# First block's decay factors built as two products outward from its middle, and one transfer of pair 1's x moved to the GpSimd queue

## Chip, cores and metric

One core of a Trainium2 chip runs the whole kernel. The metric is device time in microseconds of one execution; the kernel before has a median of 125.06 us in 3 runs (124.92 to 125.37). One further execution was taken with the hardware profiler, and everything read from the profile below belongs to that one.

## The reference

A chunked state-space scan (4 batches, 8 heads, 768 tokens, head size 32, state size 16) is followed by a bilinear feed-forward layer (3072 tokens, width 256, hidden width 1536). Cut to what matters:

```python
# attention part, chunk by chunk; the state is carried over
cum = np.cumsum(log(a)[chunk]);  L = exp(cum[i] - cum[j]) * causal
y = ((C @ B.T) * L) @ x + (C @ state) * exp(cum)
state = exp(sum(log a)) * state + sum_j B_j x_j exp(cum[-1] - cum[j])
# feed-forward part
x = y.transpose(0, 2, 1, 3).reshape(B * S, H * D)
out = ((x @ w_a) * (x @ w_b)) @ w_out
```

The decay between two tokens of a block is a ratio of running products of `a`, so B is scaled by one factor for each token and head, and C by the inverse of that factor.

## The kernel before

The 768 tokens are cut into six blocks of 128, and each block into two pairs of batches, so there are 12 pairs. For a pair the steps are: scale B and C by their factors (`scale_bc`, giving `bm` and `cm`), turn both on TensorE (`transposes`), copy them out of PSUM (`bt` by ScalarE, `ct` by VectorE or ScalarE), multiply them head by head (`scores`), mask with the causal triangle (`mask`), multiply by the scaled x (`scale_x`, `pv_u`, `pv`), and put the result into `X2T`. Then come the feed-forward products against `Wa` and `Wb` (`units_mm`, `unit`), their product `hk` (`times`) and the output product with `Wo`.

The order on each engine is written out by hand (the schedule is manual): the order of the calls in the program is the order of the instructions on every engine and on every DMA queue. A DMA issued by GpSimd stands between GpSimd's own computing instructions, one issued by SyncE (SP) or ScalarE between theirs. Eight semaphores are used in turn for the DMAs that GpSimd issues, so its ninth DMA waits until its first has landed, and so on.

What lies around the change:

- The first block's factors. `scan(0, 1)` (line 236) multiplies `a` up along 128 tokens for the 32 rows (batch, head), `over_mid` (line 239) takes the inverse of the product at token 63, and `first_factors` (lines 242 and 246) multiplies the two and turns the 32x128 result into token-major order with four turns of 32x64. That gives C's factors (`fC`); their inverse (line 761) gives B's (`fB`).
- The loads at the start. SP and ScalarE load `a`, pair 0's B, C and x. GpSimd issues pair 1's B and C, then `Wa` (first half of its columns, in two transfers: rows `f` = 0 and 1), one half of pair 1's x, and `Wb` in the same two transfers. SP issues the other half of pair 1's x, held back by a manual dependency until the factor inverse at line 761 has run, and then the constant `c32`.
- The warm-up products (line 224): products of a zeroed tile, 11 of them at the start, and some more between the first steps.
- Pair 0's first feed-forward products (line 628): `units_mm` with `Wa` and then with `Wb`, first with the upper 128 features (`f` = 0), then with the lower.
- `hr`, `hs`, `hsx` (lines 830 to 832): the decays of whole blocks, worked out between two `times` calls.

Of the kernel before, what the change touches and what calls it, by code (L numbers as in the profile page):

```python
# [10 lines left out]
f32 = mybir.dt.float32  # L11
# [3 lines left out]
ALU = mybir.AluOpType  # L15
# [14 lines left out]
def kernel(  # L30
# [13 lines left out]
    nc = tc.nc  # L44

    nb, H, S, D = x.shape
    N = B.shape[-1]
    Q = 128
# [50 lines left out]
    NE = P0 // NBP  # L99
    fB = big.tile([128, NE, 2, NBP, H], f32, name="fB")  # L100
    fC = big.tile([128, NE, H + 4 * NBP * H], f32, name="fC")
    Pe = big.tile([BH, 2, 64], f32, name="Pe")
    selr = big.tile([BH, 2, NBP, H], f32, name="selr")
    NL = NBLK - P0 // NBP
    Ps = big.tile([BH, NL, Q], f32, name="Ps")
# [27 lines left out]
    def bank(name):  # L133
        return psf.tile([128, 512], f32, name=name, tag=f"ff{next(banks)}")
# [11 lines left out]
    def load1(eng, p, which, bt, i0=0, n=64):  # L146
        blk, bp = divmod(p, NBP)
        if p >= P0:
            return eng.dma_start(
                by_token(pair_in[p][which])[:, bt],  # L150
                (B, C, x)[which][2 * bp + bt, :, blk * Q : (blk + 1) * Q, :].rearrange("h q n -> q h n"),
            )
        src = (B, C, x)[which][2 * bp + bt, :, blk * Q + 2 * i0 : blk * Q + 2 * i0 + 2 * n, :]
        return eng.dma_start(
            pair_in[p][which][64 * bt + i0 : 64 * bt + i0 + n].rearrange("i h r n -> i h (r n)"),
            src.rearrange("h (i r) n -> i h (r n)", r=2),
        )
# [10 lines left out]
    def load_w(W, t, f=None):  # L168
        src = (moe_w_a if W is Wa else moe_w_b).rearrange("(f p) e -> p f e", p=128)[:, :, t * KC : (t + 1) * KC]
        fs = slice(0, 2) if f is None else slice(f, f + 1)  # L170
        return nc.gpsimd.dma_start(W[t][:, fs], src[:, fs])
# [25 lines left out]
    nc.vector.memset(ident, 1.0)  # L197
    nc.vector.memset(causal, 1.0)
    nc.vector.memset(zero, 0.0)
    nc.vector.memset(hsx, 0.0)  # L200
    nc.vector.memset(causal_q, 1.0)
    nc.vector.memset(c32, 0.0)
    x1 = load1(nc.sync, 1, 2, 0)
    nc.sync.dma_start(c32[0:BH], p32_t.ap())
    nc.gpsimd.affine_select(
        out=ident, in_=ident, compare_op=ALU.is_equal, fill=0.0, base=0, pattern=[[-1, 128]], channel_multiplier=1
    )
# [7 lines left out]
            load1(nc.gpsimd, 1, w, bt)  # L215
    load_w(Wa, 0, 0)
    load_w(Wa, 0, 1)
    load1(nc.gpsimd, 1, 2, 1)
    load_w(Wb, 0, 0)
    load_w(Wb, 0, 1)  # L220

    def warmup(n, bank, reps=4):
        for _ in range(n):
            nc.tensor.matmul(
                bank[:, 0 : 128 * reps],
                warm,
                warm.unsqueeze(1).broadcast_to((128, reps, 128)),
                start=True,
                stop=True,
                skip_group_check=True,  # L230
            )


    def scan(lo, hi):
        for k in range(lo, hi):
            nc.vector.tensor_tensor_scan(Pr[:, k], a_sb[:, k], zero, 1.0, ALU.mult, ALU.add)

    def over_mid(lo, hi):
        nc.vector.reciprocal(rmid[:, lo:hi], Pr[:, lo:hi, 63])

    def first_factors():
        nc.vector.tensor_scalar(Pe, Pr[:, 0].rearrange("p (i r) -> p r i", r=2), rmid[:, 0:1], None, ALU.mult)
        for bt in range(2):
            for c in range(2):
                p0 = 64 * bt + 32 * c
                nc.vector.transpose(  # L246
                    fC[p0 : p0 + 32, 0, H - H * bt : H - H * bt + 64], Pe[:, :, 32 * c : 32 * c + 32]
                )

    def second_sel():  # L250
        nc.vector.tensor_scalar(
# [21 lines left out]
    def f_c(k):  # L273
        return fC[:, k, H : H + 64].rearrange("p (r b t h) -> p r b t h", r=2, b=NBP, t=2)[:, :, :, 0]
# [32 lines left out]
    def scale_bc(p, which, eng, factor=None):  # L307
        blk, bp = divmod(p, NBP)
        name = ("bm", "cm")[which]
        if p >= P0:  # L310
            f = (fBl, fCl)[which][:, blk - P0 // NBP].rearrange("p (b t h) -> p b t h", b=NBP, t=2)[:, bp]
        else:
            f = (f_c(blk) if which else fB[:, blk])[:, :, bp]
        raw = by_token(pair_in[p][which]) if p >= P0 else pair_in[p][which].rearrange("p h r n -> p r h n")
        m_ = pre.tile([128, 2, H, N], f16, name=name, tag=name)
        eng.tensor_tensor(
            out=m_,
            in0=raw,
            in1=(f if factor is None else factor).unsqueeze(3).broadcast_to((128, 2, H, N)),
            op=ALU.mult,  # L320
        )
        st.setdefault(p, {})[name] = m_
    def transposes(p, ps=None, between=None, apart=False):
        s = st[p]
        if p >= P0:
            ps = [bank("tr").bitcast(f16)] * 2
            TB, TC = ps[0][:, 0:256], ps[0][:, 256:512]
            on_dve = False
        elif ps is None:
            ps = [bank("tb") if p == 1 else SC[0], SC[1]] if apart else None  # L330
            on_dve = apart
            TB, TC = (TT[:, 0:256], TT[:, 256:512]) if ps is None else [t_.bitcast(f16)[:, 0:256] for t_ in ps]
        else:
            on_dve = True
            TB, TC = [t_.bitcast(f16)[:, 0:256] for t_ in ps]
        BT = mid.tile([128, 2, 2, 2, 64], f16, name="bt", tag="bt")
        CT = mid.tile([128, 2, Q], f16, name="ct", tag="ct")
        b_ = []

        def turn(T_, src):  # L340
            for r in range(2):
                nc.tensor.transpose(T_[:, r * 128 : (r + 1) * 128], src[:, r].rearrange("p h n -> p (h n)"), ident)  # L342

        def copy_bt(e):
            o_ = BT[:, e].rearrange("p r t i -> p (r t i)")
            b_.append(nc.scalar.activation(out=o_, in_=TB, func=AF.Copy, scale=par[:, e : e + 1]))  # L346

        turn(TB, s["bm"])
        if between:
            between()  # L350
        turn(TC, s["cm"])
        copy_bt(0)
        copy_bt(1)
        if p >= P0:
            nc.scalar.copy(CT.rearrange("p t q -> p (t q)"), TC)
            s["BT"], s["CT"] = BT.rearrange("p e r t i -> p e r (t i)"), CT
            return
        c_ = (nc.vector.tensor_copy if on_dve else nc.scalar.copy)(
            CT.rearrange("p t (i r) -> p r (t i)", r=2), TC.rearrange("p (r c) -> p r c", r=2)
        )  # L360
        if apart:
            for i_ in b_:
                tc.declare_no_dep(c_.ins, i_.ins.name, reason="reads of two banks")
        s["BT"], s["CT"] = BT, CT
# [54 lines left out]
    def mask(out_in, by_pool=False):  # L419
        o_, i_, c_ = out_in  # L420
        if by_pool:
            tmp = mid.tile([128, *c_.shape[1:]], f32, name="tmp", tag="tmp")
            nc.scalar.copy(tmp, i_)  # L423
            nc.gpsimd.tensor_tensor(out=o_, in0=tmp, in1=c_, op=ALU.mult)  # L424
        else:
            nc.vector.tensor_tensor(out=o_, in0=i_, in1=c_, op=ALU.mult)  # L426
# [198 lines left out]
    def units_mm(p, k2s, W, ps, f, ks):  # L625
        for j in ks:
            k2, t_, kk = k2s[j // 2], ps[j // 2], j % 2
            nc.tensor.matmul(  # L628
                t_[:, kk * 2 * Q : (kk + 1) * 2 * Q],
                w_up(W, 2 * k2 + kk, f),  # L630
                X2T[:, p, :, f],
                start=(f == 0 and kk == 0),
                stop=(f == 1),
                skip_group_check=True,
            )
# [117 lines left out]
    def pull(p):  # L753
        if ("S", p) in st:
            st[p].update(st.pop(("S", p)))

    warmup(11, SC[3])
    scan(0, 1)
    over_mid(0, 1)
    first_factors()  # L760
    f0 = nc.vector.reciprocal(fB[:, 0, :, 0], f_c(0)[:, :, 0])
    tc.add_manual_dep(x1.ins, f0.ins.name, AFTER, reason="x of pair 1 behind x of pair 0")
    scale_bc(0, 0, nc.vector)
    scale_bc(0, 1, nc.vector)
    scan(1, 2)
    tb, tcp = bank("tb"), bank("tc")
# [14 lines left out]
    mask(product0(1, 0))  # L781
    mask(product0(1, 1))
    scale_bc(1, 1, nc.gpsimd)
    load_w(Wa, 1)
    load_w(Wb, 1)
    nc.gpsimd.affine_select(
        out=causal_q, in_=causal_q, compare_op=ALU.is_ge, fill=0.0, base=0, pattern=[[1, Q]], channel_multiplier=-1
    )
    warmup(4, tb)
    py = [bank("py0"), bank("py1")]  # L790

# [1 line left out]
    for bt in range(2):  # L793
        evac0(0, bt, nc.scalar, py)
    transposes(1, apart=True)
    pv_u(0, 1, py, True)
    for bt in range(2):
        evac0(1, bt, nc.scalar, py)
    scan(3, 5)
    aps = [bank("aps") for _ in range(3)]  # L800
    units_mm(0, range(3), Wa, aps, 0, range(2))
    scores(1)
    mask(product(1, 3), by_pool=True)
    units_mm(0, range(3), Wa, aps, 0, range(2, 6))
    units_mm(0, range(3), Wa, aps, 1, range(6))
    asb = [evac_a(aps[0])]
# [20 lines left out]
    units_mm(0, range(3), Wb, bps, 1, range(6))  # L827
    nc.scalar.copy(maskbd, headm.unsqueeze(2).broadcast_to((128, H, D)))
    times(0, 0, bps[0], asb[0])
    nc.vector.tensor_tensor(out=hr, in0=Pr[:, 0:NG, Q - 1], in1=rmid[:, 0:NG], op=ALU.mult)  # L830
    nc.vector.tensor_tensor(out=hs, in0=hr, in1=Pr[:, 1:NBLK, 63], op=ALU.mult)
    nc.vector.tensor_tensor(
        out=hsx[0:BH],
# [246 lines left out]
```

## Time and profile before

| | |
|---|---|
| median of 3 runs | 125.06 us (124.92 to 125.37) |
| the profiled execution's own time | 125.11 us |
| its span in the profile | 123.4 us |
| TensorE (PE) busy | 117.3 us, 95% of the span |
| VectorE (DVE) busy | 91.0 us, 74% |
| ScalarE (ACT) busy | 75.7 us, 61% |
| GpSimd (POOL) busy | 61.2 us, 50% |
| granted TensorE clock | 1.0 |

The span runs from the first to the last instruction of the profile; 1.7 us of the execution's own time lie around it. The page's slices show TensorE at 90% or more nearly everywhere after the first tenth of the span. The DMA engines are busy at 70% or more from about 3 us to 68 us, and nearly idle behind that.

### The profile page before, as it was taken

The numbers are of one execution on the slowest core, as the hardware profiler recorded it, in microseconds if no ns is written. First come the engines' busy times: TensorE is split into PE (matmuls) and PEld (weight loads), VectorE is DVE, ScalarE is ACT, GpSimd is POOL, SyncE is SP. The second block draws the span as 40 slices with busy tenths as digits, with TensorE's granted clock in tenths as the row PEclk, the third lists the DMA queues.
The fourth block names the chain that finished last, engine by engine and source line by source line (L and its number), as shares of the span: only waits on it lengthen the run. The fifth ranks groups of instructions, "written<-read, shape, count | busy, mean of one in ns | idle before, by whom it ended". The sixth has DMA issues, their size and how long they took to land.

```text
span 123.4 us, 3704 instructions
## 1 busy us (share of the span) xinstructions
PE 117.3 (95%) x1456; PEld 80.0 (65%) x1456; DVE 91.0 (74%) x182; ACT 75.7 (61%) x158; POOL 61.2 (50%) x88
## 2 busy tenths in 40 slices
PE   6799799999999999999999999999999999999990
PEld 2345669889898798744477465757464775555890
DVE  3999598973995979799986988996889544747200
ACT  0447846837669866987669767457637746657220
POOL 7997989099492994097996970056000000000000
PEclk9999999999999999999999999999999999999999
DMA  3999999978899989799977601011101012010122
GB/s 66 195 155 210 185 198 204 164 137 77 89 125 115 108 111 103 91 118 93 129 271 169 204 5 45 5 43 45 43 0 43 5 43 88 0 48 0 43 85 85
DMA packets 56401, 12.15 MB, mean 99 GB/s; under 512 B 51168, under 2 KB 55936, under 8 KB 56384
## 3 DMA queue, kind: packets, MB, share of 16 engines
q1 hardware_dynamic: 51808, 7.43, 36.3%
q0 software_dynamic: 2304, 4.06, 17.4%
q10 hardware_dynamic: 2272, 0.43, 1.8%
q8 instruction: 11, 0.18, 0.6%
q14 instruction: 6, 0.05, 0.1%
HBM read 11.13 MB, written 3.15 MB: 116 GB/s over the span
## 4 chain that ended last, share of the span: by engine, by line
PE 85%; DMA 7%; DVE 5%; issue 1%; ACT 0%; DVEq 0%
PE ops L718 17%; PE aps L693 17%; PE bps L693 16%; PE ops L661 9%; PE aps L615 8%; PE bps L615 7%; DMA Wb<-in_moe_w_b_dram 5%; PE SC L372 2%; PE SC L432 2%; PE tr L342 2%; DMA a_sb<-in_a_dram 2%; DVE hk L646 1%; PE bps L628 1%; PE SC L447 1%; PE SC L522 1%; DVE fC L246 1%
## 5 line engine op out<-in xcount | busy, mean ns | idle before, releaser
L639 ACT COPY asb<-aps 128x512 f32<-128x512 f32 x72 | 41.9, 587 | 16.0 <-PE aps L693 10.4
L703 DVE TENSOR_TENSOR hkb<-bps,asb 128x512 f16<-128x512 f32 x48 | 32.3, 688 | 11.8 <-ACT asb L639 10.4
L693 PE MATMUL aps<-XB,Wa 128*128 128x512 f16 x96 | 28.6, 379 | 0.0
L693 PE MATMUL bps<-XB,Wb 128*128 128x512 f16 x96 | 28.5, 379 | 0.0
L718 PE MATMUL ops<-Wo,hkb 128*128 128x256 f16 (+1 forms) x204 | 22.8, 267 | 0.0
L718 PEld LDWEIGHTS <-hkb 128*128 128x128 f16 x204 | 18.4, 98 | 3.0
L426 DVE TENSOR_TENSOR t<-SC,causal_q 128x512 f16<-128x512 f32 x27 | 17.3, 681 | 2.2 <-PE SC L372 2.2
L646 DVE TENSOR_TENSOR hk<-bps,asb 128x512 f16<-128x512 f32 x24 | 15.6, 681 | 3.5 <-ACT asb L639 2.1
L693 PEld LDWEIGHTS <-Wb 128*128 128x128 f16 x96 | 9.9, 103 | 11.0 <-issue 0.2
L693 PEld LDWEIGHTS <-Wa 128*128 128x128 f16 x96 | 9.7, 104 | 9.2 <-issue 0.3
L730 ACT ACTIVATE osb<-ops 128x256 f32<-128x256 f32 (+1 forms) x16 | 6.0, 376 | 12.7 <-PE ops L718 12.6
L615 PE MATMUL bps<-X2T,Wb 128*128 128x256 f16 x84 | 12.6, 273 | 0.1
L615 PE MATMUL aps<-X2T,Wa 128*128 128x256 f16 x84 | 12.5, 273 | 0.2 <-DVE hk L646 0.2
L305 POOL TENSOR_SCALAR x<-xn 128x512 f16<-128x512 f32 x8 | 11.9, 1489 | 0.7
L661 PE MATMUL ops<-Wo,hk 128*128 128x256 f16 x96 | 11.7, 273 | 0.0
L661 PEld LDWEIGHTS <-hk 128*128 128x128 f16 x96 | 9.0, 98 | 1.2
L615 PEld LDWEIGHTS <-Wb 128*128 128x128 f16 x84 | 8.5, 103 | 1.1 <-issue 0.5
L615 PEld LDWEIGHTS <-Wa 128*128 128x128 f16 x84 | 8.4, 104 | 1.2 <-issue 0.5
L424 POOL TENSOR_TENSOR t<-tmp,causal_q 128x512 f16<-128x512 f32 x5 | 5.8, 1156 | 6.2 <-ACT tmp L423 6.1
L426 DVE TENSOR_TENSOR t<-SC,causal 128x512 f16<-128x512 f32 x13 | 8.2, 678 | 0.3 <-PE SC L387 0.2
L595 POOL TENSOR_TENSOR spair<-U,ch 128x128 f16<-128x128 f32 x8 | 3.1, 398 | 10.3 <-DVE U L579 10.3
L346 ACT ACTIVATE bt<-tr,ch 128x256 f16<-128x256 f16 x16 | 6.7, 472 | 0.5 <-PE tr L342 0.5
(101 smaller groups left out, 136.1 us busy)
## 6 DMA issues: line engine op xcount, KB each, us to landing
out_dram<-osb SPq DMA_DIRECT2D x23, 128.0 KB, 1.8
xn<-in_x_dram SPq DMA_DIRECT2D x5, 256.0 KB, 4.6
cn<-in_C_dram SPq DMA_DIRECT2D x8, 128.0 KB, 4.3
bn<-in_B_dram SPq DMA_DIRECT2D x8, 128.0 KB, 4.7
Wo<-in_moe_w_out_dram POOLq DMA_DIRECT2D x2, 384.0 KB, 5.9
xn<-in_x_dram POOLq DMA_DIRECT2D x3, 256.0 KB, 4.8
Wa<-in_moe_w_a_dram POOLq DMA_DIRECT2D x2, 192.0 KB, 5.5
xn<-in_x_dram SPq DMA_DIRECT2D x3, 128.0 KB, 3.5
```

The source lines that it names most:

```text
L305: eng.tensor_scalar(xo, xi, XS, None, ALU.mult)
L346: b_.append(nc.scalar.activation(out=o_, in_=TB, func=AF.Copy, scale=par[:, e : e + 1]))
L424: nc.gpsimd.tensor_tensor(out=o_, in0=tmp, in1=c_, op=ALU.mult)
L426: nc.vector.tensor_tensor(out=o_, in0=i_, in1=c_, op=ALU.mult)
L615: nc.tensor.matmul(ps[:, kk * 2 * Q : (kk + 1) * 2 * Q], w_up(W, k, f), X2T[:, p, :, f], start=(f == 0), stop=(f == 1), skip_group_check=True,
L639: (nc.vector.tensor_copy if on_dve else nc.scalar.copy)(asb, a_ps)
L646: nc.vector.tensor_tensor(out=s["hk"][:, 2 * k2 : 2 * k2 + 2, :].rearrange("p k q -> p (k q)"), in0=b_ps, in1=asb, op=ALU.mult)
L661: nc.tensor.matmul(o_ps[:, 0:d_model], hk[:, k, bt * Q : (bt + 1) * Q], Wo[:, k, :], start=(k == 0), stop=(k == NK - 1), skip_group_check= ...
L693: nc.tensor.matmul(t_, w_up(W, k, f), XB[:, blk - P0 // NBP, f].rearrange("p t j q -> p (t j q)"), start=(f == 0), stop=(f == 1), skip_gro ...
L703: return lambda: nc.vector.tensor_tensor(out=s["hk"][:, k], in0=ps[1], in1=asb, op=ALU.mult)
L718: nc.tensor.matmul(o_ps[:, 0:w], hk[:, k, c * Q : (c + 1) * Q], Wo[:, k, cs], start=(k == 0), stop=(k == NK - 1), skip_group_check=True,)
L730: nc.scalar.activation(out=o_sb[:, 0:w], in_=o_ps[:, 0:w], func=AF.Copy, scale=1.0 / (YS * YS))
```

## The change

The first block's factors are no longer built from one product along 128 tokens. Two scans of about half the length run outward from the block's middle: one forward over tokens 64 to 127 (`Pf`), one backward over tokens 63 down to 1 (`Pi`, upper 32 rows), and the inverse of the first goes into the lower 32 rows of `Pi`. The two halves of the block so lie on 64 partitions, and two turns of 64x64 take the place of four of 32x64. What is turned is now B's factor; the inverse that is taken afterwards is C's, so B is scaled before the inverse and C after it. A memset for `Pi`'s last column is added, and `hr`'s first column is copied from `Pf`.

In the queues, the half of pair 1's x that SP issued goes to GpSimd, between the other half and `Wb`'s first transfer; the manual dependency now holds back the constant `c32` instead. `Wb`'s second transfer moves behind GpSimd's scaling of pair 1's B and C. The triangle `causal_q` is made by GpSimd after its mask of pair 1 and not before it. TensorE does 10 warm-up products at the start and not 11, and pair 0's first two products with `Wa` go ahead of the second half of pair 0's `pv_u` and not behind it.

```diff
+    nc.vector.memset(Pi[0:BH], 1.0)
...
-    x1 = load1(nc.sync, 1, 2, 0)
-    nc.sync.dma_start(c32[0:BH], p32_t.ap())
+    c1 = nc.sync.dma_start(c32[0:BH], p32_t.ap())
...
     load_w(Wa, 0, 0)
     load_w(Wa, 0, 1)
-    load1(nc.gpsimd, 1, 2, 1)
+    for bt in (1, 0):
+        load1(nc.gpsimd, 1, 2, bt)
     load_w(Wb, 0, 0)
-    load_w(Wb, 0, 1)
...
     def first_factors():
-        nc.vector.tensor_scalar(Pe, Pr[:, 0].rearrange("p (i r) -> p r i", r=2), rmid[:, 0:1], None, ALU.mult)
+        nc.vector.tensor_tensor_scan(Pf[BH:64], a_sb[:, 0, 64:128], zero[:, 0:64], 1.0, ALU.mult, ALU.add)
+        nc.vector.tensor_tensor_scan(
+            Pi[0:BH, 0:63][:, ::-1], a_sb[:, 0, 1:64][:, ::-1], zero[:, 0:63], 1.0, ALU.mult, ALU.add
+        )
+        nc.vector.reciprocal(Pi[BH:64], Pf[BH:64])
         for bt in range(2):
-            for c in range(2):
-                p0 = 64 * bt + 32 * c
-                nc.vector.transpose(
-                    fC[p0 : p0 + 32, 0, H - H * bt : H - H * bt + 64], Pe[:, :, 32 * c : 32 * c + 32]
-                )
+            c0 = H - H * bt
+            nc.vector.transpose(
+                fC[64 * bt : 64 * bt + 64, 0, c0 : c0 + 64], Pi.rearrange("p (i r) -> p r i", r=2)
+            )
...
-            f = (f_c(blk) if which else fB[:, blk])[:, :, bp]
+            f = (f_c(blk) if which == (blk > 0) else fB[:, blk])[:, :, bp]
...
-    warmup(11, SC[3])
-    scan(0, 1)
-    over_mid(0, 1)
+    warmup(10, SC[3])
     first_factors()
+    scale_bc(0, 0, nc.vector)
     f0 = nc.vector.reciprocal(fB[:, 0, :, 0], f_c(0)[:, :, 0])
-    tc.add_manual_dep(x1.ins, f0.ins.name, AFTER, reason="x of pair 1 behind x of pair 0")
-    scale_bc(0, 0, nc.vector)
+    tc.add_manual_dep(c1.ins, f0.ins.name, AFTER, reason="constant behind x of pair 0")
     scale_bc(0, 1, nc.vector)
...
     scale_bc(1, 1, nc.gpsimd)
+    load_w(Wb, 0, 1)
     load_w(Wa, 1)
     load_w(Wb, 1)
-    nc.gpsimd.affine_select(
-        out=causal_q, in_=causal_q, compare_op=ALU.is_ge, fill=0.0, base=0, pattern=[[1, Q]], channel_multiplier=-1
-    )
...
     transposes(1, apart=True)
+    aps = [bank("aps")]
+    units_mm(0, range(1), Wa, aps, 0, range(2))
     pv_u(0, 1, py, True)
...
-    aps = [bank("aps") for _ in range(3)]
-    units_mm(0, range(3), Wa, aps, 0, range(2))
     scores(1)
     mask(product(1, 3), by_pool=True)
+    nc.gpsimd.affine_select(
+        out=causal_q, in_=causal_q, compare_op=ALU.is_ge, fill=0.0, base=0, pattern=[[1, Q]], channel_multiplier=-1
+    )
+    aps += [bank("aps") for _ in range(2)]
...
-    nc.vector.tensor_tensor(out=hr, in0=Pr[:, 0:NG, Q - 1], in1=rmid[:, 0:NG], op=ALU.mult)
+    nc.vector.tensor_copy(hr[:, 0:1], Pf[BH : 2 * BH, 63:64])
+    nc.vector.tensor_tensor(out=hr[:, 1:], in0=Pr[:, 1:NG, Q - 1], in1=rmid[:, 1:NG], op=ALU.mult)
```

More of the change, by code (lines that the diff above doesn't have):

```diff
@@ L101 @@
     fC = big.tile([128, NE, H + 4 * NBP * H], f32, name="fC")
-    Pe = big.tile([BH, 2, 64], f32, name="Pe")
+    Pf = big.tile([64, 64], f32, name="Pf")
+    Pi = big.tile([64, 64], f32, name="Pi")
     selr = big.tile([BH, 2, NBP, H], f32, name="selr")
```

## Prediction

> **What bounds the kernel now.** I read the page first, then the chain of waits in order of time up to 17.5 us, then the busy time in chosen stretches, then the DMA issues one by one. The page says that TensorE is the bound:
>
> ```profile
> PE 117.3 (95%) x1456; PEld 80.0 (65%) x1456; DVE 91.0 (74%) x182; ACT 75.7 (61%) x158; POOL 61.2 (50%) x88
> ```
>
> So an edit in the first 17 us can only win what TensorE idles there. The chain of waits, with start, duration and work, shows where that is:
>
> ```profile
> 0.79 2.09 DMA a_sb<-in_a_dram
> ...
> 4.93 0.26 DVE fB L761
> ...
> 5.22 0.43 DVE bm L316
> ...
> 6.36 0.44 DVE ct L358
> ...
> 6.91 6.16 DMA Wb<-in_moe_w_b_dram
> ...
> 13.12 0.62 PE bps L628 x4
> ...
> 15.05 0.69 DVE hk L646
> 15.74 0.07 DVE hr L830
> ...
> 16.12 0.69 DVE hk L646
> ...
> 16.85 0.60 PE aps L615 x4
> ```
>
> The reader is to see a seam at 6.91. GpSimd's timeline has DMA issues without a gap from 2.21 to 8.04 us, so `Wb`'s issue at 6.91 follows GpSimd's own queue and not VectorE's `ct`: what stands above the seam, the factors that the change shortens, does not set the landing at 13.07. The stretches show what the landing costs (columns: stretch, length, busy time of each engine, clock, DMA share, GB/s):
>
> ```profile
> 9.50:12.40 2.90, 2.76 (x62) 1.54 (x60) 2.70 (x7) 2.22 (x7) 2.15 (x4) 1.00 1.19 209
> 12.40:13.12 0.72, 0.01 (x2) 0.01 (x1) 0.72 (x2) 0.72 (x3) 0.72 (x2) 1.00 0.89 143
> ...
> 15.20:16.90 1.70, 1.42 (x11) 0.81 (x10) 1.63 (x6) 0.59 (x1) 1.70 (x3) 1.00 1.12 230
> 16.90:24.00 7.10, 7.10 (x96) 6.48 (x96) 6.47 (x15) 4.89 (x10) 4.36 (x7) 1.00 1.02 185
> ```
>
> TensorE is empty for 0.71 us before `Wb`, loses 0.28 more between 15.2 and 16.9 waiting for VectorE's `hk`, and is full from 16.9 on. The DMA share near or above 1 says that landings are a matter of turns on full engines. The DMA issues (one narrow window for each; last column: us from issue to landing):
>
> ```profile
> cn<-in_C_dram POOLq DMA_DIRECT2D x1, 64.0 KB, 3.5
> Wa<-in_moe_w_a_dram POOLq DMA_DIRECT2D x1, 192.0 KB, 5.1
> xn<-in_x_dram SPq DMA_DIRECT2D x1, 128.0 KB, 6.6
> Wa<-in_moe_w_a_dram POOLq DMA_DIRECT2D x1, 192.0 KB, 5.8
> xn<-in_x_dram POOLq DMA_DIRECT2D x1, 128.0 KB, 6.1
> Wb<-in_moe_w_b_dram POOLq DMA_DIRECT2D x1, 192.0 KB, 6.2
> Wb<-in_moe_w_b_dram POOLq DMA_DIRECT2D x1, 192.0 KB, 6.6
> Wa<-in_moe_w_a_dram POOLq DMA_DIRECT2D x1, 384.0 KB, 6.9
> ```
>
> The timeline has their issues at 4.44, 5.12, 5.21 (SP), 5.68, 6.20, 6.91, 7.44 and 9.25. GpSimd's queue so lands pair 1's last C at 7.9, `Wa` at 10.2 and 11.5, x at 12.3, `Wb` at 13.1 and 14.0, the next `Wa` at 16.2: steps of 2.3, 1.3, 0.8, 0.8, 0.9 and 2.1 (384 KB) us. SP's x lands at 11.8.
>
> **The factors.** Removed from VectorE, up to `bm`: scan 0.41, inverse 0.15, product 0.27, four turns of 0.235, inverse 0.25, with gaps 2.98 to 5.22, or 2.24 us. Added: two scans of 64; between the fixed 0.15 of the smallest VectorE rows and the 0.40 of 128 columns, I take the middle, 0.27 each. One inverse of 32x64: rows are 0.15 for 1 column, 0.23 to 0.25 for 16 and 0.33 to 0.35 for 32, about 0.006 us a column, so 0.5 (bounds 0.34 and 0.7). Two turns of 64x64: 0.235 for 64 columns and 0.30 for 128 are mostly fixed cost, so 0.24 each (0.47 if rows count). Sum 0.54 + 0.5 + 0.48 and 0.1 of gaps: `bm` starts near 4.6, 0.6 earlier. `cm` now stands behind the inverse (0.25), near 5.2 instead of 5.56. `bt` on ScalarE is ready earlier, but the table load (4.24 for 1.28) and the landing of `ch` (issued 2.65, 3.0 to landing) hold it to about 5.7 against 6.03. All of pair 0's first steps, `ct`, scores and masks, come about 0.35 earlier; if the bounds all go wrong, no earlier. The x of pair 0 still ends its scaling at 8.34, just behind the first two masks, so 0.3 of it reaches `pv_u`.
>
> What hides it: TensorE then comes to `Wb` at about 12.0 instead of 12.40, and only waits longer. Worth 0 by itself; without the wait it would be worth up to 0.4. The tenth warm-up fewer (about 0.4 of 4.04 us) ends near 4.7, ahead of the first turn near 5.0, so costs nothing; the memset (0.07) ends before `a` lands at 2.88.
>
> **The queues.** GpSimd issues pair 1's other x (0.77) and leaves out one `Wb` (0.56) ahead of its scaling, so `bm` and `cm` of pair 1 come about 0.2 later (8.3 and 8.9); the `Wb` and two more issues behind them end at about 11.5 instead of 10.74. GpSimd then waited 0.74 for its mask at 11.80, so the mask holds; `causal_q` (0.31) behind it delays pair 2's loads, which queue on full engines and meet a wait of 0.48 at 18.3. The ninth GpSimd DMA is now `Wb`'s first; it waits for pair 1's first B, landed at 5.5, before its issue near 7.7. `c32` goes out near 5.3, needed at 16.0. All nothing.
>
> What counts is `Wb`'s landing. While SP's x was in flight, `Wa`'s two transfers took 2.3 and 1.3 us; after it, equal transfers took about 1.0. The excess, some 1.6, is the price of that x beside the queue, at most (part of the 2.3 may be the queue's start). Inside the queue an equal x took 0.8. By steps: 7.95 + 3 x 1.03 + 2 x 0.8 = 12.6. The other end is 13.1, if total work decides; below, 12.0, if x alone costs 0.5. I take 12.7, next to the sum by steps: TensorE resumes 0.37 earlier. Pair 1's masks end at 12.95 and its scaled x at 13.12 at the latest, before `pv(1)` would start at 13.3, so nothing new is late. `Wb`'s second transfer, issued near 9.5, has its turn 1.0 behind the first, at 13.7; TensorE wants it 1.2 us behind the first (14.31 against 13.12).
>
> The Trainium skill, DMA: Bandwidth & Descriptors, section Latency and other measured facts, speaks against this move: two of the DMA engines are usually slower, by its guess because descriptors of GpSimd's DMAs are fetched from rings behind the same ports, which SP's DMAs do not use. By it x costs more in GpSimd's queue than on SP's, and `Wb` lands later, the third rival; the trace's 0.8 against up to 1.6 does not bear it out so far.
>
> **Two `Wa` products earlier.** They need `Wa`'s first transfer, at 10.2 before. Without SP's x it lands between 9.1 and 10.2; the masks before `pv_u(0, 1)` end near 9.55, so the swap costs 0 to 0.4, ahead of the wait for `Wb`: nothing.
>
> **`hr`.** The added copy stands on the chain between two `hk` at 15.74 to 16.12. Small independent VectorE instructions follow each other by 0.05 to 0.10, dependent ones by 0.18: +0.07, all on the path.
>
> **Sum.** -0.37 + 0.07 = -0.30 on the profiled execution's 125.11 (span 123.4 and 1.7 around it), which lies 0.05 above the median of the runs; so 124.8 less 0.05, rounded to 124.7.
>
> **Rivals.** First, *total work decides*: a byte on SP's queue and one on GpSimd's use the same engines, `Wb` still lands at 13.07, and the change does not do what it says: +0.07, 125.1. For it: DMA share at or above 1 from 6 us on. Against: the long steps of 2.3 and 1.3. The Trainium skill, same page, Issuing engines are not separate DMA queues, says that all queues run on the same engines and interleave, which would give this.
>
> Second, *the wait goes altogether*: x alone costs 0.5, `Wb` lands by 12.0, TensorE runs on from about 12.0: -1.1 + 0.07, so 124.0.
>
> Third, *slower turns*: `Wb` waits for a whole x at 0.8 more, and nothing returns from `Wa`: 13.9, +0.87, 125.9. It decides as soon as `Wb` lands after 13.07. For it: the first x on GpSimd's queue needed 6.1 us to land.
>
> Fourth, *landing counts from the issue*: `Wb`'s second transfer lands 6.6 behind an issue at 9.5, at 16.1 where TensorE wants it at 14.5: +1.6, 126.7. It decides if it lands more than 1.2 behind the first. Against it: the next `Wa` was issued 1.8 behind `Wb`'s second transfer and landed 2.1 behind it, which is the time of its own 384 KB and leaves none for the later issue.
>
> **Chances.** Forecast 0.50 (own range 124.3 to 125.0), total work 0.20, wait gone 0.15, slower turns 0.08, landing from issue 0.07. A measurement of this kernel can tell about 0.5%, 0.6 us, from no change. Faster than that: the wait gone, and a quarter of the forecast, 0.27; slower: the last two, 0.15; the rest 0.58. The range takes the second rival at one end and most of the third at the other, 124.0 to 125.8.
>
> **What would show it.** Right: `bm` near 4.6, `Wa`'s transfers landing about 1.0 apart and earlier, `Wb` at 12.6 to 12.8, TensorE still waiting for it, `hr`'s copy of about 0.07 between the `hk`. Wrong: `Wb` at 13.07 or later, a wait for its second transfer, TensorE waiting for `Wa` before `pv_u(0, 1)` and reaching `Wb` after it has landed, or no gap of TensorE at all.

## The result and the profile after

The changed kernel takes 125.94 us (124.83 to 127.14, 22 runs), the kernel before 124.98 us in 22 runs beside it: a ratio of 1.0068 (95% interval 1.0049 to 1.0088). Two repeats gave 1.0074 (1.0045 to 1.0103) and 1.0060 (1.0037 to 1.0083). Here and below the median is of all runs, while the ratio and its interval leave out slow runs, those over 1.5% above the fastest of their kernel. So the change costs about 0.7%, where 124.7 us, or 0.3% less than before, was forecast.

In the first profiled execution of the changed kernel (127.14 us) the clock was halved for a while, which the last section tells of, so the lines that answer to those of before come from a second profile of the same kernel (own time 126.19 us, span 124.5, clock 1.0). The page's busy times have hardly moved:

```profile
PE 117.4 (94%) x1455; PEld 80.2 (64%) x1455; DVE 91.2 (73%) x182; ACT 75.7 (61%) x158; POOL 62.1 (50%) x89
```

TensorE works 117.4 us as against 117.3, in a span that is 1.1 us longer: the loss is idle time. The chain of waits of that profile (start, duration, work):

```profile
6.93 0.76 POOL xn L155
7.69 0.23 POOL Wb L172
...
8.33 0.62 POOL bm L320
8.95 0.52 POOL cm L320
9.47 5.85 DMA Wb<-in_moe_w_b_dram
15.33 0.05 issue
15.37 0.84 PE bps L632 x6
...
17.25 0.69 DVE hk L650
17.94 0.04 issue
17.98 0.60 PE aps L619 x4
```

Before, the chain led through `Wb`'s first transfer, which landed at 13.07. Now it leads along GpSimd's own queue, through both scalings of pair 1, to the second transfer of `Wb`, which lands at 15.33. TensorE's timeline of the same profile (start, duration, work, then the idle time ahead and what ended it) has both transfers:

```profile
12.48 0.62 PE L632 MATMUL bps<-X2T,Wb 128*128 128x256 f16 x4 [0.43 <-DMA Wb<-in_moe_w_b_dram]
...
15.37 0.84 PE L632 MATMUL bps<-X2T,Wb 128*128 128x256 f16 x6 [1.29 <-DMA Wb<-in_moe_w_b_dram]
17.98 0.27 PE L619 MATMUL aps<-X2T,Wa 128*128 128x256 f16 x1 [0.76 <-DVE hk L650]
```

The lines of before that answer to the first and the last of these:

```profile
13.12 0.62 PE L628 MATMUL bps<-X2T,Wb 128*128 128x256 f16 x4 [0.71 <-DMA Wb<-in_moe_w_b_dram]
...
16.85 0.60 PE L615 MATMUL aps<-X2T,Wa 128*128 128x256 f16 x4 [0.16 <-DVE hk L646]
```

The wait for the first transfer has shrunk from 0.71 to 0.43 us, a wait of 1.29 has come up for the second, and the wait for VectorE's `hk` has grown from 0.16 to 0.76. (The prediction puts all 0.28 that TensorE lost there before down to `hk`; the timeline gives 0.16 to it, and 0.12 to a stall told of in 13.) The DMA issues in a window around 9.5 us give the second transfer's time from issue to landing:

```profile
Wb<-in_moe_w_b_dram POOLq DMA_DIRECT2D x1, 192.0 KB, 5.9
```

It is issued at 9.47, 1.9 behind the first, and lands 2.9 behind it.

### The profile page after: what moved, and what is told of

It is laid out like the page before. It is cut to its first block, busy times and chain, and to the rows that moved or that the text cites. A ratio compares the mean times of both kernels' runs of the same rounds, so it can differ in the third digit from the quotient of the medians.

```text
span 125.4 us, 3703 instructions
## 1 busy us (share of the span) xinstructions
PE 118.6 (95%) x1455; PEld 80.8 (64%) x1455; DVE 91.3 (73%) x182; ACT 75.7 (60%) x158; POOL 62.0 (49%) x89
## 4 chain that ended last, share of the span: by engine, by line
PE 84%; POOL 6%; DMA 5%; DVE 1%; issue 1%; ACT 0%
PE ops L722 17%; PE aps L697 17%; PE bps L697 16%; PE ops L665 9%; PE aps L619 8%; PE bps L619 8%; DMA Wb<-in_moe_w_b_dram 5%; PE SC L376 2%; PE SC L436 2%; PE tr L346 2%; POOL bn L155 1%; PE bps L632 1%; POOL cn L155 1%; POOL xn L155 1%; POOL Wa L172 1%; PE SC L526 1%
## 5 line engine op out<-in xcount | busy, mean ns | idle before, releaser
L734 ACT ACTIVATE osb<-ops 128x256 f32<-128x256 f32 (+1 forms) x16 | 6.0, 376 | 12.7 <-PE ops L722 12.6
L619 PE MATMUL aps<-X2T,Wa 128*128 128x256 f16 x84 | 13.2, 284 | 0.0
```

The lines of the kernel that those rows point to most:

```text
L619: nc.tensor.matmul(ps[:, kk * 2 * Q : (kk + 1) * 2 * Q], w_up(W, k, f), X2T[:, p, :, f], start=(f == 0), stop=(f == 1), skip_group_check=True,
L734: nc.scalar.activation(out=o_sb[:, 0:w], in_=o_ps[:, 0:w], func=AF.Copy, scale=1.0 / (YS * YS))
```

## The experiments

"Before" is taken beside each kernel on the same chip; its medians lay between 124.75 and 125.0 us. Line numbers differ by a few between kernels. `Wb`'s two transfers are called the first and the second.

**1. The changed kernel and the kernel before, once more.** No edit.

> The changed kernel unaltered, for a second profile on the chip on which its parts are taken back. Theory A (late issue of Wb's second transfer on top of a later bm and cm of pair 1 and the copy for hr): time 125.4 to 126.2, with floor runs near 124.9 in which TensorE does not wait for that transfer; in the profile 0.3 us more between the first two hk, and a landing of that transfer 1 to 3 us behind the first.

1.0074, 125.78 us, as expected; its profile is the one above.

> The kernel before unaltered, for a second profile of it, since the first execution profiled (125.11 us) lies above the median of all its runs (124.75). Theory: in a usual run Wb's first transfer lands by about 12.6 and TensorE waits for it 0.3 us or less; the span is 122.8 to 123.1. Rival (the wait of 0.71 us that the prediction built on is in every run): Wb lands at 13.0 to 13.1 again, span 123.4.

124.52 us in this execution, span 122.8, as the theory has it. TensorE's timeline:

```profile
12.51 0.62 PE L628 MATMUL bps<-X2T,Wb 128*128 128x256 f16 x4 [0.27 <-DMA Wb<-in_moe_w_b_dram]
...
15.90 0.51 PE L615 MATMUL bps<-X2T,Wb 128*128 128x256 f16 x3 [0.45 <-issue]
```

Unchanged, the kernel before waits 0.27 us for `Wb` here and not 0.71: the first transfer landed at 12.46, not 13.07. The wait on which the forecast's gain rested differs by 0.44 us between two executions of one program.

**2. `Wb`'s second transfer issued early again**, the rest of the change kept.

```diff
     load_w(Wb, 0, 0)
+    load_w(Wb, 0, 1)
...
     scale_bc(1, 1, nc.gpsimd)
-    load_w(Wb, 0, 1)
```

> The changed kernel with one edit undone: Wb's second transfer is issued ahead of GpSimd's scaling of pair 1 again. Theory A (the late issue of that transfer costs the time: in the changed kernel it was issued at 9.45 us, landed at 15.68, and TensorE waited 1.53 us for it): issued near 8.2 it lands within 1.2 us of the first, near 13.6 to 14.0, TensorE does not wait for it, and the time falls to 124.6 to 125.0, at or below the kernel before. Theory B (x through GpSimd's queue slows the queue for good, whatever the place of the issue): it still lands 2 us or more behind the first, and the time stays near 125.9.

1.0038 (1.0018 to 1.0059), 125.1 us: Theory A has the landing right (0.9 behind the first) and the time too low. There is no wait for `Wb` at all. The waits of TensorE up to 24 us (for what, total, times, longest) show what comes instead:

```profile
PE aps L620 <- DVE hk L651: 0.8, 1, 0.8
PE tb L347 <- POOL bm L321: 0.7, 1, 0.7
```

One more issue stands ahead of GpSimd's scaling: `bm` of pair 1 starts at 8.88 and not at 8.3, and TensorE waits for it. So the late issue is not worth nothing, but taking it back returns only about half of the loss.

**3. The late issue alone, on the kernel before.**

```diff
     load_w(Wb, 0, 0)
-    load_w(Wb, 0, 1)
...
     scale_bc(1, 1, nc.gpsimd)
+    load_w(Wb, 0, 1)
```

> The kernel before with one edit of the change alone: Wb's second transfer is issued behind GpSimd's scaling of pair 1. Theory A: it is issued near 9.3, lands near 15.5 where TensorE wants it at 14.3, TensorE waits 0.8 to 1.5 us for it, and the time is 125.6 to 126.5. Theory B: with x on SP's queue the transfer lands near 14.1 as in the kernel before, and the time stays at 125.0.

1.0027 (1.0003 to 1.0052), 125.28 us. TensorE's timeline of its profile:

```profile
14.97 0.84 PE L627 MATMUL bps<-X2T,Wb 128*128 128x256 f16 x6 [0.67 <-DMA Wb<-in_moe_w_b_dram]
```

The second transfer landed 2.3 behind the first, and TensorE waited 0.67 us: Theory A's wait, somewhat shorter, and a time below its range. Four of the twelve runs lie at 124.53 to 124.62 and eight at 125.19 to 125.60: the edit costs either nothing or some 0.7 us.

**4. The x half back on SP, the late issue kept** (the changed kernel with its first queue edit undone).

```diff
-    c1 = nc.sync.dma_start(c32[0:BH], p32_t.ap())
+    x1 = load1(nc.sync, 1, 2, 0)
+    nc.sync.dma_start(c32[0:BH], p32_t.ap())
...
-    for bt in (1, 0):
-        load1(nc.gpsimd, 1, 2, bt)
+    load1(nc.gpsimd, 1, 2, 1)
```

> The changed kernel with one edit undone: the second half of pair 1's x is issued by SP again, behind the factor inverse, and the constant behind it. Wb's second transfer stays late. Theory A: time 125.5 to 126.5, with a wait of TensorE for Wb's second transfer of 0.5 us or more. Theory B: that transfer lands within 1.2 us of the first, and the time falls to 125.0.

1.0024 (0.9994 to 1.0053), 124.88 us, with runs from 124.33 to 126.05. In the profile the second transfer, issued at 8.95, landed 4.7 later and 1.4 behind the first. That is neither expectation: TensorE did not wait for it, but three of the twelve runs take as long as Theory A has it. In this profile TensorE waits for `Wa` ahead of the two products that the change had moved forward:

```profile
9.66 0.40 PE L632 MATMUL aps<-X2T,Wa 128*128 128x256 f16 x2 [0.31 <-DMA Wa<-in_moe_w_a_dram]
```

**5. The x half in GpSimd's queue alone, on the kernel before** (the reverse of 4).

> The kernel before with one edit of the change alone: pair 1's other half of x through GpSimd's queue ahead of Wb, the constant held back instead; Wb's second transfer stays ahead of the scaling. Theory A, with the step of the prediction on Wb's first transfer: that lands at 12.4 to 12.8 instead of 13.07, the second within 1.2 us of it, time 124.6 to 124.9. Theory B: second transfer 2 us or more behind the first, time 125.6 to 126.2. A third view, that the total work on the DMA engines decides: first transfer at 13.0 to 13.1 and time 125.0.

1.0020 (1.0000 to 1.0039), 124.86 us, eight of twelve runs within 124.83 to 124.87, while the fastest runs of before lie at 124.4 to 124.5. GpSimd's timeline has `bm` of pair 1 at 8.87 (8.11 before), and TensorE's waits have

```profile
PE tb L342 <- POOL bm L316: 0.4, 1, 0.4
```

The time is Theory A's, but its step on `Wb` is not borne out: in the one profile, the slowest of the twelve runs, the first transfer landed at 13.68, the second 1.0 behind it.

**6. The late issue in between**, to separate the moment of the issue from the issue as such.

```diff
     scale_bc(1, 0, nc.gpsimd)
+    load_w(Wb, 0, 1)
     scale_x(0, nc.scalar)
...
     scale_bc(1, 1, nc.gpsimd)
-    load_w(Wb, 0, 1)
```

> The changed kernel with Wb's second transfer issued between GpSimd's two scalings of pair 1, near 8.9 instead of 9.45, and cm of pair 1 0.6 later. Theory (landing counts from the issue): it lands 0.5 us earlier than in the changed kernel, 14.6 to 15.1, where TensorE now wants it near 14.2, and the later cm costs 0.2 to 0.3: time 125.3 to 125.8. Rival (its turn follows the first transfer's once the issue is early enough): within 1.2 us of the first, 125.0 to 125.2.

1.0046 (1.0021 to 1.0071), 125.16 us. The DMA issue at 8.89:

```profile
Wb<-in_moe_w_b_dram POOLq DMA_DIRECT2D x1, 192.0 KB, 4.3
```

and TensorE's timeline:

```profile
10.19 0.28 PE L346 MATMUL SC<-ident,cm 128*128 128x128 f16 x2 [0.90 <-POOL cm L320]
...
14.10 1.05 PE L632 MATMUL bps<-X2T,Wb 128*128 128x256 f16 x8
```

Issued 0.58 earlier than in the changed kernel's second profile, the transfer landed 2.1 earlier, 0.9 behind the first, and nothing waits for it; the same time from the issue, 5.9, would have moved it by 0.58 alone. So the rival's expectation came out. But now `cm` is late, and the run gains little. (The changed kernel's third profile, in 10, limits this reading: there too the landing came early, 4.4 from the issue.)

**7. The next weights taken out of the way**: `load_w(Wa, 1)` and `load_w(Wb, 1)` of the changed kernel moved behind GpSimd's mask of pair 1; a single execution.

> The changed kernel with the transfers that follow Wb's second one (the second halves of Wa and Wb) issued behind GpSimd's mask of pair 1, near 13.1 instead of 10.0; only the landing of Wb's second transfer is looked at, the time itself suffers from the late weights. Theory (the landing counts from its own issue, 5.4 to 6.6 us in the runs so far, whatever follows): issued near 9.5 it still lands at 15.0 to 15.7. Rival (its turn is shared with the transfers behind it in the queue): with nothing behind it, it lands by 14.0, about 1.0 to 1.5 behind the first.

The execution took 127.15 us. The second transfer landed 5.2 from its issue at 9.47, 1.8 behind the first, between the two expectations. The busy time between the two landings (columns as before) says more:

```profile
12.81:14.65 1.84, 1.61 (x70) 1.06 (x70) 0.83 (x3) 1.63 (x4) 1.84 (x4) 1.00 0.14 13
```

The DMA engines are busy for 0.14 of that stretch and move 13 GB/s. So in this execution a late landing needed neither transfers behind it nor full engines; what was late was the last piece of the transfer.

**8. An issue delayed by other work, and its control.** Two triangle selects of GpSimd (some 0.6 us) are put ahead of the second transfer's issue in the kernel of 4; in the control the same work is done, but that transfer is issued early.

```diff
     scale_bc(1, 1, nc.gpsimd)
+    nc.gpsimd.affine_select(out=causal_q, ...)
+    nc.gpsimd.affine_select(out=causal_q, ...)
     load_w(Wb, 0, 1)
```

> The changed kernel with x of pair 1 half on SP, and the issue of Wb's second transfer delayed by about 0.6 us of GpSimd work (the triangle causal_q made there, twice), to about 9.5 us instead of 8.95. Theory (an issue later than about 9.2 us finds its turn gone, wherever x lies): it lands 2 us or more behind the first, near 14.5 to 15.3, and the time is 125.2 to 125.8. Rival (x in GpSimd's queue is needed for the late landing): it lands within 1.4 us of the first, as in the run with x on SP, time 124.6 to 125.0.

> The control: the same 0.6 us of GpSimd work at the same place, x half on SP, but Wb's second transfer issued ahead of the scaling, near 7.5 us. Theory: it lands within 1.2 us of the first, TensorE waits 0.3 us or less, time 124.7 to 125.1 as for the kernel of the factors alone. Rival (the later issue of the weights behind it costs as much): 125.3 or more.

Delayed: 1.0027 (1.0002 to 1.0053), 125.32 us. Control: 0.9987 (0.9960 to 1.0014), 124.79 us. So the late issue costs 0.4% by the two ratios, whose intervals just overlap. The time is the theory's, and that of the control the control's theory. Yet in the profiled execution, one of the quickest of its runs (124.91), there is no such wait: the transfer was issued at 9.62 and landed 4.1 later, 1.45 behind the first, and the products of its half follow on at once.

```profile
13.54 1.08 PE L632 MATMUL bps<-X2T,Wb 128*128 128x256 f16 x8
```

**9. `hr`'s copy taken off the path**, the rest of the change kept.

```diff
     over_mid(2, NBLK)
+    nc.vector.tensor_copy(hr[:, 0:1], Pf[BH : 2 * BH, 63:64])
...
     times(0, 0, bps[0], asb[0])
-    nc.vector.tensor_copy(hr[:, 0:1], Pf[BH : 2 * BH, 63:64])
```

> The changed kernel with the copy into hr's first column moved ahead of the first hk, into VectorE's idle time behind the block inverses. Theory: the start of the second hk comes 1.07 us behind the start of the first as in the kernel before, not 1.37, and the time is 0.3 us below the changed kernel's. Rival (the copy is a small independent instruction worth 0.07 on the path, as the prediction had it): 0.07 us below.

1.0041 (1.0021 to 1.0062), 125.38 us, against 1.0074 for the changed kernel on the same chip. That is 0.4 us below it by the medians, where the theory had 0.3. In its profiled execution (127.13 us, longer than all its others) the two `hk` start 1.07 apart, as before the change; the second transfer lands late (6.0 from its issue) and TensorE waits 1.58 us for it. The landing does not hang on the copy.

**10. Both taken back at once**, beside the changed kernel and the kernel of 2 on one chip: this tells whether the two costs add or cover each other. The edit is that of 2 with that of 9.

> The changed kernel with Wb's second transfer issued early again and hr's copy moved ahead of the first hk; x of pair 1 stays in GpSimd's queue. Theory, the two costs add: the copy is worth 0.3% and the late issue 0.3%, each taken alone, so from 1.007 the ratio comes to about 1.001, and what is left is x in GpSimd's queue against the shorter factors. Rival, the two cover each other (with one taken away the other wait moves to the front): no better than either alone, 1.004. A ratio under 1.0025 speaks for the first, over it for the second.

> The changed kernel with Wb's second transfer issued early, once more: 1.004 by both theories, and 0.3% below the changed kernel beside it if the late issue costs what was read before.

> The changed kernel once more, on the same chip as its two part-way versions, so that the differences are taken there: 1.007 by both theories. If it comes out under 1.005 the loss itself depends on the chip.

1.0020 (1.0003 to 1.0038), 1.0032 (1.0008 to 1.0056) and 1.0060 (1.0037 to 1.0083). The order is that of two costs that add, and 1.0020 lies on that side of the 1.0025 set beforehand; but its interval reaches over it, and the step from 1.0020 to 1.0032 is smaller than the intervals. The copy's share is plainer in the fastest runs: with it, five of twelve lie within 125.08 to 125.11, without it four within 124.80 to 124.89. VectorE's timeline with the copy in its place:

```profile
14.78 0.69 DVE L651 TENSOR_TENSOR hk<-bps,asb 128x512 f16<-128x512 f32 x1 [0.55 <-ACT X2T L515]
15.50 0.14 DVE L834 COPY hr<-Pf 32x1 f32<-32x1 f32 x1
15.68 0.15 DVE L835 TENSOR_TENSOR hr<-Pr,rmid 32x4 f32<-32x4 f32 x1
15.86 0.16 DVE L836 TENSOR_TENSOR hs<-hr,Pr 32x5 f32<-32x5 f32 x1
16.06 0.17 DVE L837 TENSOR_TENSOR hsx<-hs,c 32x20 f32<-32x20 f32 x1
16.15 1.27 DVE L651 TENSOR_TENSOR hk<-bps,asb 128x512 f16<-128x512 f32 x2
```

and with the copy ahead of the first `hk`:

```profile
14.26 0.14 DVE L818 COPY hr<-Pf 32x1 f32<-32x1 f32 x1
14.77 0.69 DVE L651 TENSOR_TENSOR hk<-bps,asb 128x512 f16<-128x512 f32 x1 [0.38 <-ACT X2T L515]
15.38 0.14 DVE L835 TENSOR_TENSOR hr<-Pr,rmid 32x4 f32<-32x4 f32 x1
...
15.85 1.27 DVE L651 TENSOR_TENSOR hk<-bps,asb 128x512 f16<-128x512 f32 x2
```

From `hk` to `hk` it is 1.37 with the copy and 1.08 without: 0.29 us. The product for `hr` begins 0.08 before the `hk` ahead of it has ended; the copy begins 0.03 behind that end, and the product waits 0.18 behind the copy.

The third profile of the changed kernel fell on the quickest of its seven runs (124.98 us). TensorE's timeline:

```profile
12.75 0.62 PE L632 MATMUL bps<-X2T,Wb 128*128 128x256 f16 x4 [0.71 <-DMA Wb<-in_moe_w_b_dram]
...
13.95 1.05 PE L632 MATMUL bps<-X2T,Wb 128*128 128x256 f16 x8
```

The second transfer, issued at 9.47 as always, here took 4.4 and landed 1.1 behind the first, and nothing waited for it. The same program, the same issue, and a landing 1.5 to 1.8 us earlier than in its two other profiles.

**11. The factors alone**: the changed kernel with both queue edits undone (4 and 2 together), the copy in its place.

> The changed kernel with both queue edits undone: x of pair 1 half on SP, Wb's second transfer ahead of the scaling. The factors, the order of TensorE and the copy for hr stay. Theory (in a usual run TensorE does not wait for Wb, so the shorter factor chain is on the path): -0.35 for the factors and +0.3 for the copy, 124.6 to 124.8 against 124.75. Rival (the prediction's: the factors are covered by the wait for Wb): 0.1 to 0.3 above the kernel before, 124.9 to 125.1.

1.0024 (1.0007 to 1.0041), 125.13 us, above both expectations and nearest to the rival's; `hk` to `hk` is 1.37.

**12. The factors with all of `hr`, `hs`, `hsx` ahead of the first `hk`** (11, and the group moved behind `over_mid(2, NBLK)`), run twice; this was the candidate to beat both kernels.

> The kernel of the factors alone, with all four small instructions of hr, hs and hsx moved ahead of the first hk. Theory: they run in VectorE's idle time (1.25 us in the kernel before), the second hk follows the first at once, 0.68 us earlier than with the copy on the path, unless TensorE's bps or ScalarE's asb becomes the last: 124.0 to 124.3, below the kernel before. Rival: the second hk then waits for something else as long, 124.6 or more.

> The kernel of the factors alone with hr, hs and hsx ahead of the first hk, once more, for an interval. Theory: 0.2 to 0.3 us below the kernel before. Rival: the first measurement was luck, no difference within 0.1 us.

0.9981 (0.9954 to 1.0009), 124.53 us, and 0.9987 (0.9964 to 1.0010), 124.79 us. The first falls between its two expectations, the second is 0.2 below the kernel before by the medians. Neither interval leaves out 1: the best version found is not shown to be faster than before.

**13. That move alone, on the kernel before.**

> The kernel before with one edit of no part of the change: the three small instructions of hr, hs and hsx moved ahead of the first hk, into VectorE's idle time. Theory: the second hk follows the first at once, 0.38 us earlier, TensorE's wait of 0.16 to 0.28 us there goes, and the time is 124.3 to 124.5 against 124.75. Rival: TensorE is bound there by its own products, time 124.7.

0.9990 (0.9972 to 1.0007), 124.78 us: the expected 0.38 us did not come. TensorE's timeline has a gap elsewhere:

```profile
15.96 0.51 PE L615 MATMUL bps<-X2T,Wb 128*128 128x256 f16 x3 [0.46 <-issue]
```

The unaltered kernel has the same gap of 0.45 in 1. Six of the twenty profiles have such a stall, of 0.06 to 0.95 us, always among the same four matmuls: the two of before, 11, both of 12, and this one. In these six a transfer of 16 KB that the trace counts as instructions ends between 14.4 and 15.2 us, and TensorE goes on 1.3 to 1.5 us behind its end; in the other fourteen it ends by 14.3, and there is no stall. No run was made to move that transfer, so this is a coincidence in time and not a cause shown; but where TensorE stalls there, as here, time won ahead of the stall need not come out behind it.

## Why the prediction was wrong, point by point

Undone one by one, the parts make a ladder from before to after: x in GpSimd's queue 1.0020 (5), with the factors and the small edits 1.0020 (10), with the copy on the path 1.0032 and 1.0038 (10 and 2), with the late issue 1.0060 to 1.0074. The order is read from medians: the steps are of the size of the intervals; what the traces show at each carries the reading.

**The step that failed** is "`Wb`'s second transfer, issued near 9.5, has its turn 1.0 behind the first, at 13.7", priced at nothing. Issue and landing in nine profiles, seven with a later issue and, for comparison, two with an early one (us; the next columns count from the issue and from the first transfer's landing). The trace notes the arrival of a transfer in sixteen parts, and the landing is the last of them; the last column says how many had arrived by 14.0 us:

| kernel | x half | issue | landing | from issue | behind the first | parts by 14.0 |
|---|---|---|---|---|---|---|
| changed, first profile | GpSimd | 9.45 | 15.68 | 6.2 | 3.1 | 13 |
| changed, second | GpSimd | 9.47 | 15.33 | 5.9 | 2.9 | 14 |
| changed, third | GpSimd | 9.47 | 13.84 | 4.4 | 1.1 | 16 |
| copy off the path (9) | GpSimd | 9.46 | 15.43 | 6.0 | 3.4 | 13 |
| late issue alone (3) | SP | 9.63 | 14.92 | 5.3 | 2.3 | 15 |
| x back on SP (4) | SP | 8.95 | 13.61 | 4.7 | 1.4 | 16 |
| issue delayed (8) | SP | 9.62 | 13.74 | 4.1 | 1.45 | 16 |
| issue in between (6) | GpSimd | 8.89 | 13.23 | 4.3 | 0.9 | 16 |
| issued early (2) | GpSimd | 8.15 | 13.62 | 5.5 | 0.9 | 16 |

Each row is one execution. Issued by 8.9, it came 0.9 to 1.0 behind the first in all twelve profiles that there are (the two of before among them), as the prediction had it. Issued from 9.4 on, it came anywhere from 1.1 to 3.4 behind, where the prediction wanted it within 1.2. The whole transfer did not lose its turn: in the four rows that land behind 14.9, 13 to 15 of the sixteen parts were there by 14.0, close to the forecast 13.7, and one to three came 0.1 to 1.7 later (in 7 fifteen were there, and the last came at 14.65). So a late issue does not move the landing by a fixed amount, it makes it uncertain. The run times say the same: of the changed kernel's 38 runs 25 took over 125.5 us, of the 24 with the early issue (2 and 10) five, of before's 165 nine. In its best runs (124.71, 124.83 and 124.98 in the three sets) the changed kernel is ahead of the version with the early issue (125.04 at best), because pair 1's `bm` is 0.56 earlier; in most it loses that and more. The measured 125.94 is the 125.9 of the third rival, but that is luck: its sign, a first transfer landing behind 13.07, is in none of the changed kernel's three profiles. The fourth rival, at 0.07, came nearest: the wait is the one that it named. Its price of 1.6 was too high for most runs, and its mechanism, a fixed time from the issue, does not fit 4.1 to 6.2 for one size. The evidence cited against it was a transfer of 384 KB issued 1.8 behind its forerunner that landed in its own time; this one observation of one execution was taken for a rule. Why a few parts lag behind a late issue, and only in some executions, is not settled: the trace does not say which DMA engine carried which part.

**The copy for `hr`** was rightly put on the path and mis-sized: 0.07 forecast, 0.29 measured. It counted a small instruction between independent ones. The copy starts only behind the `hk` ahead of it, 0.11 later than `hr`'s product did, and the product then follows as a dependent instruction, another 0.18. TensorE's wait for that `hk` shows the same price: 0.75 to 0.76 in nine profiles with the copy on the path and 0.46 in four without it (the six with the stall of 13 and the one with the halved clock aside), where before's first profile had 0.16 behind a stall of 0.12.

**The gain of 0.37** was a difference from one execution. `Wb`'s first transfer landed at 12.4 to 12.7 in the three profiles of the changed kernel, and 12.7 was forecast; but in before's second profile it landed at 12.46 already. What was left to win was the wait of 0.27 there. Over all kernels, it landed at 12.02 to 13.07 (median 12.4) in the ten profiles with the x half on SP, and at 11.95 to 13.68 (median 12.5) in the ten with it in GpSimd's queue: no gain that stands out of the scatter. `Wa`'s two transfers did land 1.0 to 1.1 apart instead of 1.3, as forecast, but the two x behind them took that back. And the 13.07 from which the steps were reckoned was the last of sixteen parts; the fifteenth had come at 12.30. Steps between landings of one execution were taken for prices of bytes on full engines, although the DMA share in the wait itself was 0.89. So the first rival, total work decides, fits this transfer better, though not its 13.07. The Trainium skill, DMA: Bandwidth & Descriptors, section Issuing engines are not separate DMA queues, holds that all queues share the same engines; the two medians, 12.4 and 12.5, agree with it.

**GpSimd's queue.** `bm` and `cm` of pair 1 came at 8.30 and 8.89, as forecast (8.3 and 8.9). "Nothing" held only because the late issue had made room: with x in GpSimd's queue and `Wb` issued early, they come at 8.88 and 9.46, TensorE waits 0.4 to 0.8 for `bm`, and the fastest runs are nearly 0.4 slower than before's (5). In the changed kernel TensorE waits 0.29 for `cm`, ahead of its wait for `Wb`, which covers it. The change paid for the longer queue with the late issue.

**The factors** went as worked out. VectorE's timeline of the changed kernel's first profile:

```profile
3.04 0.28 DVE L243 TENSOR_TENSOR_SCAN Pf<-a_sb,zero 32x64 f32<-32x64 f32 x1 [1.18 <-DMA a_sb<-in_a_dram]
3.35 0.28 DVE L244 TENSOR_TENSOR_SCAN Pi<-a_sb,zero 32x63 f32<-32x63 f32 x1
3.65 0.54 DVE L247 RECIPROCAL Pi<-Pf 32x64 f32<-32x64 f32 x1
4.23 0.49 DVE L250 STREAM_TRANSPOSE fC<-Pi 64x64 f32<-64x64 f32 x2
4.75 0.43 DVE L320 TENSOR_TENSOR bm<-bn,fC 128x256 f16<-128x256 f32 x1
```

Scans of 0.28 (0.27 forecast), the inverse 0.54 (0.5), the turns 0.49 together (0.48), `bm` at 4.75 (4.6) as against 5.22. In the three profiles of the changed kernel TensorE is ready for `Wb` at 12.03 to 12.05 (12.0 forecast) and only waits longer. "Worth 0 by itself" agrees with the runs: 0.24% with the copy (11), whose own share is 0.23% (0.29 of 125 us), and between -0.13% and -0.19% where `hr` is off the path (12), of which that move alone makes -0.10% (13). But the wait for `Wb` is not all that hides the factors: in the profile of 11 TensorE waits 0.29 for `cm`, 0.19 for `Wa` and 0.28 for `Wb`, and meets the stall of 13.

**The small terms.** The two earlier `Wa` products cost the changed kernel no wait in its profiles; with the x half on SP they wait 0.19 to 0.31 for `Wa` (4, 8, 11), inside the 0 to 0.4 forecast. No run singles out the missing warm-up product or the moved triangle. In the sum, 125.11 - 0.30 - 0.05 is 124.76, and 124.7 a slip in rounding.

## What to carry to other kernels

Before a transfer is issued later "because its turn comes later anyway", look for its landing in several executions: an early issue is insurance, and what it costs is seen in every execution, what it saves only in those where the landing is late. A transfer has landed when its last part has, so the time between two landings of one execution is no price of their bytes. A gain that rests on one wait in one profile is worth what a second profile of the same kernel leaves of it. A tiny instruction put into a chain between two large ones costs its place in the overlap and a dependent start, here four times what its neighbours' spacing suggested.

## What the hardware did that was not expected

In the first profile of the changed kernel the clock fell to half behind the wait for `Wb`. The busy time in stretches (columns as before: stretch, length, busy time of each engine, clock, DMA share, GB/s):

```profile
12.39:15.80 3.41, 1.68 (x71) 1.14 (x72) 1.23 (x4) 2.15 (x5) 3.41 (x6) 1.00 0.99 143
15.80:19.21 3.41, 3.41 (x17) 2.44 (x18) 2.66 (x8) 0.59 (x1) 2.26 (x4) 0.50 1.13 217
```

For 3.41 us TensorE ran at 0.50, four products taking 1.06 us and not 0.60, and that execution took 127.14 us. A granted clock of 0.984 to 0.986 over the whole run, as this one's 0.985, is found in four of the changed kernel's 38 runs and one of the 24 with the early issue (2 and 10), and in none of the 143 runs of before whose clock is on record. The Trainium skill, TensorE: Matmul & The Clock Gate, Part 1: The HAM clock gate, has a window of about 3.4 us that runs freely, after an idle one of which the clock is halved. The length agrees; but TensorE was busy for 1.68 of the 3.41 us ahead, so the window was not an idle one. A wait as long (1.58 us) in 9 left the clock at 1.00.
